# The guarded sum of a softmax row, moved from VectorE to ScalarE, with a new order of instructions

## The chip, the core and the metric

The kernel runs on one core of a Trainium2 chip. The core has five engines with instruction streams of their own, which wait for each other through semaphores: TensorE (PE) does matrix products and writes them to PSUM; its weight loads (PEld) run beside its products. VectorE (DVE) does reductions and elementwise work, ScalarE (ACT) activation functions of the form f(scale * x + bias), GpSimd (POOL) elementwise work on SBUF alone, and SyncE (SP) issues transfers between HBM and SBUF. Each engine runs its instructions in the order in which they were written; what stands first and must wait holds all behind it. The metric is the time of one launch on the device, in microseconds (us), as the median of several runs.

## The reference, cut to what matters

Eight batches, eight heads, 576 tokens, 64 values a head. Attention keeps only scores within tau of the row's maximum, and its result goes through a gated network with a convolution over three tokens.

```python
scores = scale * np.matmul(q, k.transpose(0, 1, 3, 2))
thresh = np.max(scores, axis=-1, keepdims=True) - tau
scores = np.where(scores >= thresh, scores, -1000000000.0)
scores = scores - np.max(scores, axis=-1, keepdims=True)
attn = np.exp(scores)
attn = attn / (np.sum(attn, axis=-1, keepdims=True) + 1e-09)
out = np.matmul(attn, v)                 # then, per batch, on all heads side by side:
h = np.maximum(x @ w_in, 0.0)            # 512 -> 1024
conv_out = sum over k of conv_w[k] * h shifted by k - 1 tokens
y = (h / (1 + np.exp(-conv_out))) @ w_out  # 1024 -> 512
```

The change touches the divisor: the sum of a row of exponentials plus a small guard.

## The kernel before

**Tiling.** A batch is cut in two chunks of query tokens, of 256 and 320 (L40, L284). A pair of heads is handled at a time; the first half of the keys of both lies on the lower 64 of the 128 partitions, the second half on the upper 64. A *unit* is 128 rows of queries for a pair (two heads, so two score tiles of 128 x 576); the last 64 rows of two pairs share a unit. There are 144 units, 18 a batch.

**One unit** (`unit`, L548). For each head h, PE makes the scores in PSUM (L569), DVE takes the row's maximum, negated (L581), and ACT takes the exponential with that as its bias (L588) into a tile `em`. DVE makes both thresholds (L585), then per head compares the scores with the threshold and multiplies the exponentials by the outcome, adding them up on the way (mask, L591). All these scalars lie in one tile `few` of 14 columns: the two sums in columns 4 and 6, and beside each, in 5 and 7, the guard, a constant written once (L319). The *guarded sum* is a DVE reduce over the pairs (4, 5) and (6, 7) that gives both heads at once, in columns 10 and 11 (L612); DVE takes their reciprocals in place (L615), and POOL, or DVE in a sixth of the first eight units' heads, scales `em` by them (L629). There are four `few` tiles and six `em` tiles, used in turn, and two score tiles in PSUM.

**After a unit** its `em` is turned so that keys lie on partitions: in 60 units by PE in blocks, with ACT copying them out of PSUM (L688, L698, L704), in 84 by splitting the words into halves on ACT and POOL (L337, L339), writing them to HBM (L666) and reading them back by two turning transfers (L673). When a group of two pairs has its turned blocks, `attend` makes the products with v (L724), ACT and DVE write them as a high and a low part (L732, L735). When a chunk has all of them, the network runs: first products (L754), Relu (L763), the two outer taps (L769), Tanh (L776), the gate (L774), high and low parts (L784, L344), second products (L805) and the copy to the output (L812). In the first stretch the weights are loaded and split as well (`split`, L365).

**The order.** No engine's order is written by hand. Each operation is registered with `op` (L102): engine, estimated ns, what it reads and writes, and `ahead`, the number of units by which it may run before its own unit's turn. `Plan.run` (L121) then plays all engines against each other: an engine that is free takes, of its operations that are ready and have a buffer, the one with the least rank minus `ahead` (L183 to L224). It uses estimates: LATENCY (from the end of an operation on one engine to its use on another), HOLD (a port shared by DVE and POOL), LATE (what is added for transfers), ALT (the handicap of an engine that is not an operation's home), and, on PE, SWITCH (cost of a change between 64-row work "rows", transposes "turn" and full-array work "full") with KEEP, how far past its due time PE may stay in the same form. The order found is the order written, on all engines at once, so one constant can shift every stream. MOE is read in `ffn` (L817) alone: how many first and second products alternate.

The lines of the sum before:

```python
        op("dve", 85, guard, w=[(few, "inverse")], r=ss, ahead=a)
        op("dve", 82, lambda: nc.vector.reciprocal(few[:, inverse], few[:, inverse]), w=[(few, "inverse")], ahead=a)
```

Of the kernel before, what the change touches and what calls it, by code (L numbers as in the profile page):

```python
# [16 lines left out]
AF = mybir.ActivationFunctionType  # L17
ALU = mybir.AluOpType
PSUM = bass.MemoryType.PSUM

LEAST = 2.0 ** -80
FEW = 4
AHEAD = {'mask': 16.335, 'norm': 7.023, 'parts': -3.757, 'gate': 1.809, 'evac': 0.518, 'low': 0.256, 's': 8.629, 's4': 9.599, 't': 3.039, 'a': 3.703, 'prep': 6.114, 'w': 0.866, 'load': 0.211, 'first': 6.092}

LATENCY = {'pe': 225.727, 'act': 201.983, 'dve': 114.993, 'pool': 52.585, 'ring': 1864.473}

HOLD = {'pool': 113.97, 'dve': 80.64}

NORM = (('pool', 'pool', 'pool', 'pool', 'pool', 'dve'), ('pool',))

# [1 line left out]
PIECES = 12  # L32
LOW = ('pool', 'pool')
HPB = 3
MOE = (2, 1)
BACKLOG = {'pool': 3000.0, 'dve': 1500.0, 'act': 9000000000.0}
WRATE = (1.997, 2.191)
ALT = 4.35

FIRST = [(0, 1), (2, 3, 4)]  # L40
GROUPS = [(0, 1), (2, 3, 4)]
# [18 lines left out]
STB = 3  # L60
ETB = 2
VAB = 3
QB = 2
CROSS = ((2, 1, 2, 1), (2, 1, 2, 1), (0, 0))
LATE = {'load': 1341.0, 'copy': 13872.0, 'rows': 132.0, 'turn': 331.0}

KEEP = {'rows': 3.312, 'cols': 0.001, 'turn': 0.039, 'full': 0.041}


class Buf:  # L70
# [184 lines left out]
def tile_tau_attention_gated_ffn(  # L255
# [13 lines left out]
    nc = tc.nc  # L269
# [34 lines left out]
    op = plan.op  # L304
# [13 lines left out]
    for x in fews:  # L318
# [3 lines left out]
            w=[(x, "tau")], r=[(x, 0), (tau_sb, 0)], ahead=8.0  # L322
# [9 lines left out]
    gate = const("gate", [P, 1], F32)  # L332
# [151 lines left out]
    ring = [const(f"g{i}", [P, NFB, RING], F32R) for i in "hl"]  # L484
# [63 lines left out]
    def unit(u, sides, small):  # L548
# [5 lines left out]
        few = plan.buf(sm, "few", FEW, [P, 14], F32, f"few_{u}")  # L554
        few.home = fews[few.turn % FEW]
        a = AHEAD["s4" if small else "s"]
        late, pss = [], []
        add = dict(op=ALU.add, axis=mybir.AxisListType.X)
        m = 2
        for h in range(m):  # L560
# [29 lines left out]
            def mask(scores=scores, th=th, view=view, total=total):  # L590
# [7 lines left out]
                r=[x for _, k, r in sides for x in ((k, h), *r(h))], ahead=a, kind="rows"  # L598
# [8 lines left out]
        ss = [(few, ("sum", h)) for h in range(m)]  # L607
        inverse = slice(10, 10 + m)
# [2 lines left out]
            pairs = few[:, 4:4 + 2 * m].rearrange("p (h two) -> p h two", two=2)  # L611
            nc.vector.tensor_reduce(few[:, inverse], pairs, **add)  # L612

        op("dve", 85, guard, w=[(few, "inverse")], r=ss, ahead=a)
        op("dve", 82, lambda: nc.vector.reciprocal(few[:, inverse], few[:, inverse]), w=[(few, "inverse")], ahead=a)  # L615
        turns = NORM[u >= NEAR]
        homes = [turns[(u * 2 + h) % len(turns)] for h in range(m)]
        if "act" in homes:
            op(
                "dve", 82, lambda: nc.vector.tensor_scalar(few[:, 12:12 + m], few[:, inverse], LEAST, None, op0=ALU.mult),  # L620
                w=[(few, "least")], r=[(few, "inverse")], ahead=a
            )
        for h, home in enumerate(homes):
# [227 lines left out]
    whole, made, vts, lasts, eTs = {}, {}, {}, {}, {}  # L851
# [8 lines left out]
    for now in range(len(units) + 1):  # L860
        plan.rank = float(now)
        if now < len(units):
            i, t, n = units[now]
# [106 lines left out]
```

## Time and profile before

| | |
|---|---|
| three timed runs | 836.83, 838.25, 838.29 us; median 838.25 |
| profiled execution | 836.68 us |
| its span, first to last instruction | 834.6 us |
| instructions | 20770 |
| mean granted clock of PE | 0.998 |
| HBM read and written | 47.34 MB, 58.98 MB |

The page of the profile and the answers drawn from its trace name an engine, a line (L612 is line 612 of the kernel), an operation with the tile that it writes and those that it reads, and a count. In a row of a group, the first number behind the bar is busy time in us, the second the mean of one instruction in ns, the third the idle time of the engine just ahead of these instructions, with what ended most of it. Operations of one engine overlap at their ends, so the length of one is more than the time for which it holds its engine; that is seen where two start one behind the other. Windows give busy times within a stretch of the span. Waits give who was waited for, the total in us, how often, and the longest. Idle time of an engine that is not the bottleneck costs nothing.

### The profile page before, as it was taken

To read this page: it belongs to the slowest core of one execution; us is meant where nothing else is said; L and a number is where in the kernel's file an instruction comes from. 1 tells how busy PE (TensorE), PEld (TensorE's weight loads), DVE (VectorE), ACT (ScalarE), POOL (GpSimd) and SP (SyncE) were. 2 spreads that over 40 slices of the span, in tenths; PEclk is the share of its full clock that TensorE was granted. 3 is DMA by queue.
4 is the path that set the end of the run, shared out by engine and by line. 5 is a ranking of instruction groups with operands and counts; after the bars stand their busy time and mean duration, and the time that the engine had idled before them with its cause. 6 is when DMAs were issued, how large, how long until landed. Compare 5 with 4: busy or idle time off the path is not lost.

```text
span 834.6 us, 20770 instructions
## 1 busy us (share of the span) xinstructions
PE 812.8 (97%) x7584; PEld 591.3 (71%) x7584; DVE 722.9 (87%) x1802; ACT 610.0 (73%) x1245; POOL 483.5 (58%) x631
## 2 busy tenths in 40 slices
PE   6889999999999999999999999999999999999998
PEld 2446767667777677767777677767777677777896
DVE  6999999989989699997989789997989879997542
ACT  5999787778777577876767777875867857776642
POOL 3456666755657357764756646674665637665321
PEclk9999999999999999999999999999999999999999
DMA  7446248999887789899898678889787887785301
GB/s 271 138 158 200 78 113 235 230 254 241 196 213 187 201 213 211 208 226 229 202 216 196 183 206 225 209 190 218 209 203 218 189 207 187 208 196 156 55 27 38
DMA packets 248550, 157.23 MB, mean 188 GB/s; under 512 B 203776, under 2 KB 222465, under 8 KB 248449
## 3 DMA queue, kind: packets, MB, share of 16 engines
q1 hardware_dynamic: 248016, 155.61, 72.5%
q8 instruction: 60, 0.98, 0.5%
q14 instruction: 42, 0.34, 0.1%
q10 hardware_dynamic: 432, 0.30, 0.1%
HBM read 47.34 MB, written 58.98 MB: 127 GB/s over the span
## 4 chain that ended last, share of the span: by engine, by line
PE 91%; DVE 4%; ACT 3%; issue 1%; POOL 0%; DMA 0%; DVEq 0%
PE po L805 24%; PE ph L754 24%; PE ps_s L569 18%; PE pa L724 16%; PE ps_t L688 7%; DVE few L581 2%; DVE em L591 1%; ACT em L588 1%; ACT eT L698 1%; DVE t L769 0%; PE pw_stage L415 0%; POOL em L629 0%; ACT stage L393 0%; ACT stage_f L389 0%; DMA k<-in_kp_dram 0%
## 5 line engine op out<-in xcount | busy, mean ns | idle before, releaser
L629 POOL TENSOR_SCALAR em<-em,few 128x576 f32<-128x576 f32 x285 | 227.0, 807 | 189.6 <-DVE few L615 147.0
L588 ACT ACTIVATE em<-ps_s,few 128x576 f32<-128x576 f32 x288 | 209.5, 744 | 68.1 <-DVE few L581 66.9
L581 DVE TENSOR_REDUCE few<-ps_s 128x1 f32<-128x576 f32 x288 | 209.2, 748 | 43.1 <-PE ps_s L569 41.3
L591 DVE SCALAR_TENSOR_TENSOR em<-ps_s,few,em 128x576 f32<-128x576 f32 x288 | 224.2, 811 | 13.1 <-ACT em L588 5.8
L754 PE MATMUL ph<-x,w1h 128*128 128x322 f32 (+1 forms) x1024 | 230.7, 304 | 0.8 <-ACT hp L763 0.8
L344 POOL TENSOR_TENSOR gl<-t,gh 128x255 fp32r<-128x255 f32 (+9 forms) x192 | 122.8, 651 | 109.1 <-ACT gh L784 102.7
L754 PEld LDWEIGHTS ph<-x,w1h 128*128 128x128 f32 x1024 | 170.6, 189 | 21.0 <-issue 15.2
L569 PE MATMUL ps_s<-k,q 64*64 64x288 f32 x2048 | 162.4, 424 | 8.5 <-DVE k L341 3.9
L724 PE MATMUL pa<-eT,v 64*64 64x256 f32 (+1 forms) x2304 | 152.5, 404 | 0.0
L754 PE MATMUL ph<-x,w1l 128*128 128x322 f32 (+1 forms) x512 | 150.9, 295 | 0.0
L724 PEld LDWEIGHTS pa<-eT,v 64*64 64x64 f32 x2304 | 88.7, 133 | 51.0 <-issue 3.2
L805 PE MATMUL po<-w2h,gh 128*128 128x512 f32 x288 | 119.2, 414 | 0.0
L569 PEld LDWEIGHTS ps_s<-k,q 64*64 64x64 f32 x2048 | 65.8, 134 | 68.5 <-issue 26.4
L805 PE MATMUL po<-w2h,gl 128*128 128x512 f32 x288 | 112.6, 391 | 0.0
L805 PE MATMUL po<-w2l,gh 128*128 128x512 f32 x288 | 112.6, 391 | 0.0
L769 DVE SCALAR_TENSOR_TENSOR t<-hp,cr 128x321 f32<-128x321 f32 (+1 forms) x128 | 88.4, 692 | 22.7 <-ACT hp L763 21.7
L339 POOL COPY parts<-em 128x1152 uint16<-128x1152 uint16 x84 | 101.9, 1213 | 3.9
L337 ACT ACTIVATE parts<-em 128x1152 uint16<-128x1152 uint16 x84 | 98.2, 1169 | 4.4 <-POOL em L629 4.1
L754 PEld LDWEIGHTS ph<-x,w1l 128*128 128x128 f32 x512 | 96.5, 188 | 0.3
L688 PE MATMUL ps_t<-ident,em 128*128 128x128 f32 x540 | 85.6, 284 | 8.7 <-ACT eT L698 5.0
L776 ACT ACTIVATE t<-t,cm 128x321 f32<-128x321 f32 (+1 forms) x128 | 68.6, 540 | 31.9 <-DVE t L769 19.9
L688 PEld LDWEIGHTS ps_t<-ident,em 128*128 128x128 f32 x540 | 61.6, 143 | 42.5 <-issue 19.7
(71 smaller groups left out, 871.7 us busy)
## 6 DMA issues: line engine op xcount, KB each, us to landing
rows<-parts SPq DMA_DIRECT2D x84, 576.0 KB, 3.6
q<-in_qd_dram SPq DMA_DIRECT2D x63, 256.0 KB, 4.0
v<-in_vc_dram SPq DMA_DIRECT2D x36, 288.0 KB, 4.4
out_dram<-ot SPq DMA_DIRECT2D x36, 256.0 KB, 3.8
k<-in_kp_dram SPq DMA_DIRECT2D x31, 288.0 KB, 4.8
stage<-in_w_in_dram SPq DMA_DIRECT2D x8, 512.0 KB, 5.3
stage<-in_w_out_dram SPq DMA_DIRECT2D x8, 512.0 KB, 4.0
eT<-rows SPq DMA_TRANSPOSE x168, 4.4
```

What stands on the lines that cost most here:

```text
L337: nc.scalar.activation(dst, src, AF.Copy, scale=scale)
L339: engines[e].tensor_copy(dst, src)
L344: engines[e].tensor_tensor(dst, x, y, op=ALU.subtract)
L569: nc.tensor.matmul(ps[g * D:(g + 1) * D, AT + c * CH:AT + (c + 1) * CH], lhsT=q(on, h), rhs=k[on, h * CH:(h + 1) * CH], start=True, stop=True)
L581: nc.vector.tensor_reduce(few[:, nm], scores(), op=ALU.max, axis=mybir.AxisListType.XY, negate=True)
L588: nc.scalar.activation(view(), scores(), AF.Exp, bias=few[:, nm])
L591: nc.vector.scalar_tensor_tensor(view(), scores(), few[:, th], view(), op0=ALU.is_ge, op1=ALU.mult, accum_out=few[:, total])
L629: engines[e].tensor_scalar(sl, sl, LEAST, few[:, 10 + h:11 + h], op0=ALU.add, op1=ALU.mult)
L688: nc.tensor.transpose(out=pt[:, i * P:(i + 1) * P], in_=block, identity=ident[:])
L724: nc.tensor.matmul(pa[j * D:(j + 1) * D, :w], lhsT=vt[on, step, :], rhs=eT[on, :w // D, step, :], start=(step == 0), stop=(step == NBLK - 1))
L754: nc.tensor.matmul(ph[:, :an], lhsT=w1[w][:, cb, fs], rhs=xs[cb][:, h, :an], start=(cb == 0 and i == 0), stop=(cb == NCB - 1 and i == 2))
L805: nc.tensor.matmul(po[:], lhsT=x[:, f, at:at + P], rhs=w[:, f, :], start=(f == 0 and i == 0), stop=(f == NFB - 1 and i == 2))
```

## The change

The sum with its guard becomes two activations, one a head: out = Identity(sum + bias), with the guard's column as the bias, written to columns 10 and 11. DVE's reciprocal then reads what both wrote. In the planner an activation is estimated at 112 ns and has a lead of `a + AHEAD["norm"]`, that is 8.629 + 5.208 units (9.615 + 5.208 in a unit of 64-row remainders). The branch on "act" in `homes` isn't reached, since NORM names POOL and DVE alone. The constants of the planner change as well: the leads in AHEAD, LATENCY, HOLD, ALT, LATE, KEEP and MOE.

```diff
-AHEAD = {'mask': 16.335, 'norm': 7.023, 'parts': -3.757, 'gate': 1.809, 'evac': 0.518, 'low': 0.256, 's': 8.629, 's4': 9.599, 't': 3.039, 'a': 3.703, 'prep': 6.114, 'w': 0.866, 'load': 0.211, 'first': 6.092}
-LATENCY = {'pe': 225.727, 'act': 201.983, 'dve': 114.993, 'pool': 52.585, 'ring': 1864.473}
-HOLD = {'pool': 113.97, 'dve': 80.64}
+AHEAD = {'mask': 18.575, 'norm': 5.208, 'parts': -4.059, 'gate': 1.956, 'evac': 0.512, 'low': 1.528, 's': 8.629, 's4': 9.615, 't': 3.024, 'a': 3.793, 'prep': 6.793, 'w': 0.762, 'load': 0.212, 'first': 6.093}
+LATENCY = {'pe': 235.362, 'act': 201.983, 'dve': 114.993, 'pool': 53.653, 'ring': 1862.277}
+HOLD = {'pool': 113.804, 'dve': 80.206}
...
-MOE = (2, 1)
+MOE = (1, 1)
-ALT = 4.35
+ALT = 6.24
...
+GUARD = "act"
-LATE = {'load': 1341.0, 'copy': 13872.0, 'rows': 132.0, 'turn': 331.0}
-KEEP = {'rows': 3.312, 'cols': 0.001, 'turn': 0.039, 'full': 0.041}
+LATE = {'load': 1389.0, 'copy': 16128.0, 'rows': 332.0, 'turn': -600}
+KEEP = {'rows': 3.535, 'cols': 0.001, 'turn': 0.02, 'full': 0.049}
...
-        op("dve", 85, guard, w=[(few, "inverse")], r=ss, ahead=a)
-        op("dve", 82, lambda: nc.vector.reciprocal(few[:, inverse], few[:, inverse]), w=[(few, "inverse")], ahead=a)
+        if GUARD == "act":
+            for h in range(m):
+                op(
+                    "act", 112, lambda h=h: nc.scalar.activation(
+                        few[:, 10 + h:11 + h], few[:, 4 + 2 * h:5 + 2 * h], AF.Identity, bias=few[:, 5 + 2 * h:6 + 2 * h]
+                    ), w=[(few, ("whole", h))], r=[(few, ("sum", h))], ahead=a + AHEAD["norm"]
+                )
+            ss = [(few, ("whole", h)) for h in range(m)]
+        else:
+            op("dve", 85, guard, w=[(few, "inverse")], r=ss, ahead=a)
+        op("dve", 82, lambda: nc.vector.reciprocal(few[:, inverse], few[:, inverse]), w=[(few, "inverse")], r=ss, ahead=a)
...
-                "dve", 82, lambda: nc.vector.tensor_scalar(few[:, 12:12 + m], few[:, inverse], LEAST, None, op0=ALU.mult),
+                "act", 110, lambda: nc.scalar.activation(few[:, 12:12 + m], few[:, inverse], AF.Copy, scale=LEAST),
```

## The prediction

> **What bounds the kernel now.** I read the busy times of the page first, then the chain that ended last, then the windows by stage, and last the waits of the stages in which TensorE (PE) is idle.
>
> ```profile
> PE 812.8 (97%) x7584; PEld 591.3 (71%) x7584; DVE 722.9 (87%) x1802; ACT 610.0 (73%) x1245; POOL 483.5 (58%) x631
> PE 91%; DVE 4%; ACT 3%; issue 1%; POOL 0%; DMA 0%; DVEq 0%
> 0.00:20.00 20.00, 11.94 (x83) 5.74 (x84) 13.51 (x38) 11.60 (x21) 6.09 (x22) 1.00 0.79 268
> 20.00:100.00 80.00, 71.76 (x673) 43.99 (x673) 77.36 (x193) 73.42 (x153) 49.67 (x55) 0.98 0.44 145
> 100.00:450.00 350.00, 349.03 (x3399) 254.74 (x3399) 319.73 (x805) 264.06 (x528) 215.96 (x275) 1.00 0.84 208
> 450.00:800.00 350.00, 348.94 (x3266) 258.94 (x3266) 297.59 (x745) 247.50 (x519) 203.89 (x273) 1.00 0.75 189
> 800.00:835.00 35.00, 31.13 (x170) 27.90 (x168) 14.69 (x24) 13.42 (x28) 7.89 (x8) 1.00 0.08 30
> ```
>
> A window row gives its length, then the busy time of PE, PE's weight loads, VectorE (DVE), ScalarE (ACT) and GpSimd (POOL), then granted clock, DMA share and GB/s. The shares of the first two rows say "PE", and the windows say where that holds. From 100 to 800 us PE is idle for 0.97 + 1.06 = 2.03 us in 700: whatever DVE gains there can only go to those 2 us and to the way in which PE's work is strung together. From 20 to 100 us it is otherwise: PE idles 8.24 us, DVE 2.64, ACT 6.58. There both are as full as PE. After 800 us the guarded sum no longer runs (its last row of the window view below), so that stretch cannot change by it.
>
> The start's own chain, by line, and the waits of the body (100 to 800 us), with us in total, number and longest:
>
> ```profile
> by line: DVE few L581 11.3%; PE pa L724 10.8%; PE ps_s L569 9.2%; DVE em L591 8.5%; ACT em L588 8.0%; PE ps_t L688 6.8%; ACT eT L698 6.1%; issue 5.8%; PE ph L754 5.8%; PE pw_stage L415 4.0%; ACT stage L393 3.6%; ACT stage_f L389 2.8%; ACT w
> PEld ps_s L569 <- issue: 23.2, 84, 0.5
> PEld ps_t L688 <- issue: 14.9, 34, 0.4
> PEld ph L754 <- issue: 14.7, 34, 0.4
> PEld po L805 <- issue: 7.3, 16, 0.5
> PEld pa L724 <- issue: 2.1, 9, 0.4
> PEld ps_t L688 <- POOL em L629: 2.5, 4, 1.1
> PE ps_t L688 <- POOL em L629: 0.7, 1, 0.7
> ```
>
> In the start the chain is a braid: DVE holds 11.3 + 8.5 = 19.8% with the row maximum and the mask, ACT at least 8.0 + 6.1 + 3.6 + 2.8 = 20.5% (the row is cut off; I take 22%). In the body what is left are 84 + 34 + 34 + 16 + 9 = 177 places where weight loads pause with nothing to wait for: there the matmul changes its form (64-row tiles, transposes, full array). What one costs PE is seen below.
>
> **The change, part by part.** Removed is the two-element reduce on DVE, once a unit; added are two one-element Identity activations a unit on ACT, and two hand-overs, DVE to ACT and back.
>
> ```profile
> L612 DVE TENSOR_REDUCE few<-few 128x2 f32<-128x4 f32 x144 | 21.4, 149 | 2.3
> 20.00:100.00 80.00, 2.12 (x14) 0.98 0.44 145
> 100.00:800.00 700.00, 18.82 (x127) 1.00 0.80 199
> 800.00:835.00 35.00, 0.00 (x0) 1.00 0.08 30
> 405.90 0.08 DVE L591 DVE_READ_ACCUMULATOR em<-ps_s,few,em 128x1 f32 x1
> 406.29 0.15 DVE L612 TENSOR_REDUCE few<-few 128x2 f32<-128x4 f32 x1
> 406.36 0.47 DVE L769 SCALAR_TENSOR_TENSOR t<-hp,cr 128x255 f32<-128x255 f32 x1
> 406.75 0.16 DVE L615 RECIPROCAL few<-few 128x2 f32<-128x2 f32 x1
> 407.09 1.64 POOL L629 TENSOR_SCALAR em<-em,few 128x576 f32<-128x576 f32 x2 [1.23 <-PE ps_s L569]
> ```
>
> The last five rows are start, length, engine and line. The reduce lasts 0.149 us, but the next operation starts 406.36 - 406.29 = 0.07 us after it: it holds DVE for 0.07, and 0.149 is the upper end. So DVE is relieved of 14 x 0.07 = 1.0 us (to 2.1) in the start and of 127 x 0.07 = 8.9 us (to 18.8) in the body.
>
> The trace has no Identity, so I build its price from what is nearest: a copy of one column, and two activations of 255 columns from the same memory, one with a per-partition operand and one without.
>
> ```profile
> L784 ACT ACTIVATE gh<-t 128x1 fp32r<-128x1 f32 x8 | 1.7, 211 | 0.1
> 529.75 0.74 ACT L588 ACTIVATE em<-ps_s,few 128x576 f32<-128x576 f32 x1
> 530.37 0.57 ACT L784 ACTIVATE gh<-t 128x1 fp32r<-128x1 f32 x2
> 398.18 0.42 ACT L784 ACTIVATE gh<-t 128x255 fp32r<-128x255 f32 x1
> 398.48 1.16 ACT L337 ACTIVATE parts<-em 128x1152 uint16<-128x1152 uint16 x1
> 409.78 0.53 ACT L776 ACTIVATE t<-t,cm 128x255 f32<-128x255 f32 x1
> 410.18 0.43 ACT L784 ACTIVATE gh<-t 128x255 fp32r<-128x255 f32 x1
> ```
>
> The 255-column copy holds ACT for 398.48 - 398.18 = 0.30 us, the Tanh, whose scale is a tile, for 410.18 - 409.78 = 0.40: the operand costs 0.10. Activations overlap: the exp lasts 0.74 and the next starts after 0.62, 0.12 earlier. A one-column copy lasts 0.211, so it holds ACT for 0.211 - 0.12 = 0.09. With the bias tile an Identity is 0.19; the ends are 0.09 (operand free) and 0.31 (0.21 + 0.10, nothing overlapped). The planner is told 0.112. ACT gets 288 x 0.19 = 54.7 us: 28 x 0.19 = 5.3 in the start (2.5 to 8.7), 254 x 0.19 = 48.3 in the body, where ACT is idle 85.94 + 102.50 = 188.4 us, so the body hides it; without that cover up to 48.3 us would be on the path.
>
> **Start, ACT.** Of 5.3 us I put on the path the share that ACT has of the start's chain, 22%: +1.2 (0 to +5.3). **Start, DVE**: 20% of 1.0: -0.2 (0 to -2.1). Before 20 us the first unit may gain or lose a few tenths by its order: 0.
>
> The Trainium skill, on the page "ScalarE: Activation LUTs", section "Rules for kernel authors", sends additions to VectorE and not to ScalarE. The rows bear it out for price (0.07 us a unit on DVE against 0.38 on ACT); by that rule alone nothing is gained and the start pays its 5.3, which is the slower rival below.
>
> **The longer hand-over.** Before, sum to reciprocal stays on DVE, and GpSimd starts the division 407.09 - 405.98 = 1.1 us after the last sum. Now an Identity pair stands between: behind it in ACT's strict order wait the next exp and the evacuations of PSUM, and behind the reciprocal on DVE wait the maxima that release exps and the masks that free the score banks. The two Identities take at least 0.19 + 0.31 = 0.5 us with their operands at hand, so division starts about 0.5 later per unit. PE felt GpSimd's division in 4 + 1 places of the body; 0.5 more in each is 2.5, most covered by the six buffers of em: +0.3 (-0.5, where the planner now sets the reciprocal sooner, to +2.5).
>
> **The body's DVE relief.** 8.9 us fewer on DVE, and masks with more lead (16.3 to 18.6 units), can take back what PE idles: of 2.0 us I take -1.6 (0 to -2.0).
>
> **The new order.** The price of one change of form on PE:
>
> ```profile
> 405.85 0.28 PE L754 MATMUL ph<-x,w1l 128*128 128x256 f32 x1
> 405.96 0.28 PE L754 MATMUL ph<-x,w1h 128*128 128x256 f32 x1
> 406.17 0.72 PE L569 MATMUL ps_s<-k,q 64*64 64x288 f32 x8
> ```
>
> Within a run the next matmul starts after 0.11, across the change after 0.21: 0.10 is lost. The planner may now stay in 64-row work 3.535 units past its due time, not 3.312, and in full-array work slightly longer. If one change in ten of the 177 goes, that is 18 x 0.10 = -1.8 (+3.5 to -3.5 for a fifth more or fewer, since nothing in the trace fixes the sign). MOE does nothing: in L829 to L833 all second-matmul items but one are already out before the loop that reads it, so its only effect is in how many first-matmul items each round takes, and their order stays. ALT prices engines other than an operation's home, and the trace has none used:
>
> ```profile
> L629 POOL TENSOR_SCALAR em<-em,few 128x576 f32<-128x576 f32 x285 | 227.0, 807 | 189.6 <-DVE few L615 147.0 <-PE ps_s L569 32.5 <-PE ps_t L688 7.1
> L629 DVE TENSOR_SCALAR em<-em,few 128x576 f32<-128x576 f32 x3 | 2.5, 834 | 0.0
> ```
>
> (285 + 3 divisions, as the homes say.) LATENCY and HOLD are estimates that only shift the order; LATE's copy is read nowhere; the ACT form of "least" isn't reached, as no home is "act".
>
> **DMA turns and loads.** LATE tells the planner that rows land 0.20 us later and turns 0.93 us earlier: attention may be put 0.73 earlier against its turned blocks. Loads of q, k and v get 0.68 unit more lead, and SP issues in order, so a load that waits for its buffer holds the turns behind it.
>
> ```profile
> eT<-rows SPq DMA_TRANSPOSE x168, 4.4
> SPq L511 <- PE ps_s L569: 34.4, 26, 3.6
> ```
>
> 168 turns are six for each of 28 attention groups; loads of q already wait 26 times for PE. Before, PE never idled ahead of pa, so I take 0 (0 to 28 x 0.73 = +20 if every group sat at its limit).
>
> **Sum.** +1.2 - 0.2 + 0.3 - 1.6 - 1.8 = -2.1. The profiled execution took 836.68 us (span 834.6 and 2.1 around it), so 834.6. The three timed runs have their median 1.57 us above it, at 838.25; carried there, 836.15, given as 836.2, which is 0.24% faster. This kernel's measurement tells about 0.2% (1.7 us) from no change; its own runs lie 1.5 apart.
>
> **Rivals.**
> - *ACT takes over the start* (slower). All 28 Identities land on the chain: 5.3 less the 1.0 of DVE, 838.25 + 4.3 = 842.5. It decides from where added ACT time plus the waits for sums exceeds ACT's 6.6 us idle there: 28 hand-overs of 0.05 each suffice. For it: ACT's 73.42 of 80 us, and a planner that counts 0.112 where rows give 0.19. Against: only a fifth of the chain is ACT's. Chance 0.19.
> - *The turns or the SP queue become a wait.* A quarter of the 0.73 in each of 28 groups is 5.1: 843.4. For it: the planner's shift; against: no wait of pa now. Chance 0.09.
> - *PE hides it all.* Body at 99.7% PE, start's plus and minus cancel: 836.6 to 839.9, nothing measurable. Chance 0.28.
> - *The order is much better.* A fifth of the form changes (-3.5), the 2.0 of idle, and a third of the start's 8.2 of PE idle (-2.7): 830.0. Chance 0.10.
> - *The change does not do what it says*, by a table load around each Identity. Chance 0.01, left out of the range:
>
> ```profile
> L330 ACT ACT_TABLE_LOAD x1 | 1.3, 1283 | 1.7 <-PEq L958 1.7
> ```
>
> One load of 1.283 us serves Exp, Tanh, Relu, Abs and Copy here; 288 of them would add some 370 us to ACT.
>
> **How the numbers follow.** The forecast, 1.7 to 5 us of gain (833.2 to 836.6), has 0.33. Faster: 0.33 + 0.10 = 0.43; same: 0.28; slower: 0.19 + 0.09 + 0.01 = 0.29. As both signs are likely, the range takes in both: 830, the better order, to 843, just above the ACT rival; a tenth is left out on either side.
>
> **What would show it.** L612 gone, 288 Identities of 0.21 to 0.31 us; DVE's busy time lower by 10 to 21 us, ACT's higher by 50 to 90. Right in its steps, if PE's idle time from 100 to 800 us falls below 2 us and the pauses by "issue" below 177. Wrong, if PE's busy time in the first 100 us falls behind 83.7 with ACT full there (first rival), if PE idles ahead of pa (second), or if the number of form changes grows.

## The result and the profile after

| | before | after |
|---|---|---|
| median of four timed runs, us | 837.95 (836.83 to 838.29) | 842.41 (841.89 to 842.94) |
| profiled execution, us | 836.68 | 842.04 |
| its span, us | 834.6 | 840.2 |

After over before is 1.0059, with a 95% interval of 1.0044 to 1.0074. The change makes the kernel slower by about 5 us. The forecast was 0.24% faster.

First the page of the kernel after: busy time by engine, and the shares of the chain that ended last.

```profile
PE 816.5 (97%) x7584; PEld 596.4 (71%) x7584; DVE 709.0 (84%) x1658; ACT 667.9 (80%) x1533; POOL 488.4 (58%) x631
PE 89%; ACT 7%; DVE 2%; POOL 1%; issue 1%; DMA 0%; ACTq 0%; DVEq 0%
```

DVE has 144 instructions fewer and is busy 13.9 us less; ACT has 288 more and is busy 57.9 us more, as foretold. In the chain ACT's share went from 3% to 7%. Where that is, the windows of the kernel after show (length, then PE, PEld, DVE, ACT, POOL, then granted clock, DMA share, GB/s):

```profile
0.00:20.00 20.00, 11.15 (x82) 5.13 (x82) 12.95 (x33) 12.55 (x26) 5.95 (x21) 1.00 0.80 270
20.00:100.00 80.00, 69.54 (x643) 40.15 (x639) 73.95 (x176) 76.28 (x174) 51.51 (x54) 0.98 0.45 142
100.00:450.00 350.00, 349.38 (x3394) 256.48 (x3390) 311.08 (x731) 290.57 (x660) 216.16 (x274) 1.00 0.81 207
450.00:800.00 350.00, 349.72 (x3289) 262.18 (x3282) 296.28 (x697) 274.52 (x645) 206.85 (x276) 1.00 0.76 191
800.00:841.00 41.00, 36.66 (x195) 32.48 (x193) 14.70 (x24) 14.02 (x29) 7.90 (x8) 1.00 0.09 33
```

From 100 to 800 us PE is idle for 0.62 + 0.28 = 0.90 us; it was 2.03. By that sign the body is better. But at 800 us PE has 36.66 us of work left, and had 31.13 before: it is 5.5 us late. In the first 100 us PE was busy 11.15 + 69.54 = 80.69 us (83.70 before), ACT 88.83 (85.02 before).

PE's network products date the loss more directly than busy time. The window 0 to 100 us of the tile ph (first products; PE, PEld, ACT, then clock, DMA share, GB/s), for the kernel before and then the one after:

```profile
0.00:100.00 100.00, 12.23 (x81) 10.24 (x81) 2.87 (x6) 0.98 0.51 170
```

```profile
0.00:100.00 100.00, 9.41 (x63) 7.88 (x63) 2.50 (x5) 0.98 0.52 167
```

And the answer on the tile po, whose two times are the first and the last start of a second product, again before and then after:

```profile
L805 PE MATMUL po<-w2h,gh x288: 387/393/504, 104.6 to 830.3; 128*128 128x512 f32 x144
```

```profile
L815 PE MATMUL po<-w2h,gh x288: 387/393/504, 110.1 to 835.8; 128*128 128x512 f32 x144
```

By 100 us PE has issued 63 matmuls of the first products where it had issued 81. The first second product comes at 110.1 and not at 104.6, the last at 835.8 and not at 830.3: 5.5 late at the one, 5.5 late at the other, with 725.7 us between them in both kernels. **The loss is there by 110 us, and the body neither adds to it nor takes any of it back.** The chain of waits in the stretch 20 to 100 us of the kernel after, by line, shows what the start now hangs on:

```profile
by line: ACT em L589 11.6%; PE pa L734 10.9%; PE ps_s L570 9.2%; ACT eT L708 9.2%; ACT stage_f L390 7.2%; ACT stage L394 5.9%; POOL stage_f L403 5.1%; PE pw_stage L416 3.9%; ACT few L618 3.8%; issue 3.5%; ACT w2h L411 3.1%; DVE cr L464 2.9%
```

ACT now holds at least 11.6 + 9.2 + 7.2 + 5.9 + 3.8 + 3.1 = 40.8% of it, twice the 20.5% of before, and the maximum and the mask on DVE have gone from its head. The Identities themselves are 3.8%. Such shares are no measure of load, though: experiments 3, 4 and 14 show how unsteady they are. What remains to be told apart is whether ACT's added time made it so, or the new order.

### The profile page after: what moved, and what is told of

Same layout as the page of the kernel before. It is cut to its first block, busy times and chain, and to the rows that moved or that the text cites. A ratio compares the mean times of both kernels' runs of the same rounds, so it can differ in the third digit from the quotient of the medians.

```text
span 840.2 us, 20888 instructions
## 1 busy us (share of the span) xinstructions
PE 816.5 (97%) x7584; PEld 596.4 (71%) x7584; DVE 709.0 (84%) x1658; ACT 667.9 (80%) x1533; POOL 488.4 (58%) x631
## 4 chain that ended last, share of the span: by engine, by line
PE 89%; ACT 7%; DVE 2%; POOL 1%; issue 1%; DMA 0%; ACTq 0%; DVEq 0%
PE ph L764 24%; PE po L815 24%; PE ps_s L570 18%; PE pa L734 15%; PE ps_t L698 7%; ACT em L589 2%; ACT eT L708 1%; ACT stage_f L390 1%; ACT stage L394 1%; ACT few L618 1%; DVE few L582 1%; ACT parts L338 1%; POOL em L639 0%; POOL stage_f L403 0%; PE pw_stage L416 0%
## 5 line engine op out<-in xcount | busy, mean ns | idle before, releaser
L639 POOL TENSOR_SCALAR em<-em,few 128x576 f32<-128x576 f32 x286 | 231.1, 819 | 190.6 <-DVE few L625 164.2
L589 ACT ACTIVATE em<-ps_s,few 128x576 f32<-128x576 f32 x288 | 207.4, 748 | 50.2 <-DVE few L582 48.5
L345 POOL TENSOR_TENSOR gl<-t,gh 128x255 fp32r<-128x255 f32 (+14 forms) x191 | 125.5, 667 | 115.4 <-ACT gh L794 105.4
L734 PEld LDWEIGHTS pa<-eT,v 64*64 64x64 f32 x2304 | 91.8, 133 | 48.4 <-issue 2.9
L570 PEld LDWEIGHTS ps_s<-k,q 64*64 64x64 f32 x2048 | 68.0, 134 | 66.2 <-issue 30.6
L338 ACT ACTIVATE parts<-em 128x1152 uint16<-128x1152 uint16 x84 | 98.3, 1170 | 16.5 <-POOL em L639 16.4
L779 DVE SCALAR_TENSOR_TENSOR t<-hp,cr 128x321 f32<-128x321 f32 (+1 forms) x128 | 84.1, 659 | 24.8 <-ACT hp L773 23.5
L618 ACT ACTIVATE few<-few 128x1 f32<-128x1 f32 x288 | 85.5, 305 | 19.4 <-DVE em L592 18.1
```

The costliest lines, as they stand in the source:

```text
L338: nc.scalar.activation(dst, src, AF.Copy, scale=scale)
L345: engines[e].tensor_tensor(dst, x, y, op=ALU.subtract)
L570: nc.tensor.matmul(ps[g * D:(g + 1) * D, AT + c * CH:AT + (c + 1) * CH], lhsT=q(on, h), rhs=k[on, h * CH:(h + 1) * CH], start=True, stop=True)
L589: nc.scalar.activation(view(), scores(), AF.Exp, bias=few[:, nm])
L639: engines[e].tensor_scalar(sl, sl, LEAST, few[:, 10 + h:11 + h], op0=ALU.add, op1=ALU.mult)
L734: nc.tensor.matmul(pa[j * D:(j + 1) * D, :w], lhsT=vt[on, step, :], rhs=eT[on, :w // D, step, :], start=(step == 0), stop=(step == NBLK - 1))
```

## The experiments

In most of them the order is *frozen*: the planner plays with one kernel's operations, estimates and constants, so all streams stay where they are, and only the instruction emitted at the place of the sum is another. So order and instruction can be told apart. All ratios are to the kernel before on the same chip, with their 95% intervals; those of the experiments come from five rounds. The numbers behind "first" and "last" are the first and last start of a second product, as in the rows above, in one profiled run each; the timed runs of one kernel lie up to 3.8 us apart (experiment 11), in most under 2, so small differences say little there.

| | sums in the start (17 units) | in the body | ratio | first to last, us |
|---|---|---|---|---|
| before | DVE | DVE | 1 | 104.6 to 830.3 |
| 3, old order | ACT | DVE | 1.0043 | 108.7 to 834.6 |
| 4, old order | DVE, and ACT loaded | DVE | 1.0044 | 108.5 to 834.0 |
| 13, old order | DVE, and ACT loaded | the same | 1.0048 | 107.6 to 834.9 |
| 9, old order | ACT | ACT | 1.0093 | 108.0 to 838.8 |
| 14, old order | no sum | no sum | 0.9981 | 103.9 to 828.1 |
| 10, new order | DVE | DVE | 1.0038 | 109.8 to 834.1 |
| 2, new order | ACT | DVE | 1.0066 | 111.8 to 836.4 |
| 1, new order | DVE | ACT | 1.0074 | 111.2 to 837.3 |
| after | ACT | ACT | 1.0059 | 110.1 to 835.8 |

### 1 and 2: the new order, with the sums of one stage back on DVE

The first of a unit's two places stays empty; at the second stands the old reduce (for all units before the 18th, or for all from it on).

```diff
...
+            seen = []
...
+            def whole_sum(h):
+                if u < 17:          # experiment 2: u >= 17
+                    seen.append(h)
+                    if len(seen) == m:
+                        guard()
+                else:
+                    nc.scalar.activation(few[:, 10 + h:11 + h], few[:, 4 + 2 * h:5 + 2 * h], AF.Identity, bias=few[:, 5 + 2 * h:6 + 2 * h])
...
```

> The changed kernel's order of instructions is kept; only in the first 17 units (those of the first 100 us) the guarded sum is the old reduce on VectorE, put where the second Identity stood. Theory 'ScalarE is the bound of the start': the 34 Identities of 0.185 us each no longer hold it, so most of the 4.4 us by which PE's work lags at 90 us comes back: about 838.0 to 839.5. Rival 'the new order itself is slower in the start': nothing comes back, 841.5 to 843. Rival 'the hand-over between VectorE and ScalarE costs it everywhere': a seventh or less comes back, 841.5 or more.

> The changed kernel's order is kept; the Identities stay in the first 17 units, and the other 127 units have the reduce on VectorE. Theory 'ScalarE is the bound of the start': the body is TensorE's, nothing changes, 841.5 to 843.0. Rival 'the hand-over costs everywhere': it is gone in 127 of 144 units, so 838 to 839. Rival 'the new order itself': 841.5 to 843 as well.

Measured: 843.22 us, 1.0074 (1.0060 to 1.0087), and 842.24 us, 1.0066 (1.0054 to 1.0078). With the body's sums on ACT, taking the Identities out of the start of the new order gives nothing back (from after to 1: +0.15%). With the body's sums on DVE the same step does give something: from 2 to experiment 10, below, 0.28%, 2.3 us. So what the start's Identities cost in the new order has no single size, and part of experiment 1's time may be the granted clock's (last section). Either way the first second product stays 5.2 to 7.2 us late, so the simple form of the first rival, 28 Identities on the start's chain, is not the whole of what the new order shows.

### 3 and 4: the old order, with ACT loaded in the start

Experiment 3 emits the two Identities where the reduce stood. Experiment 4 keeps the reduce and adds two Identities of constants into columns that nobody reads: ACT gets the time, nobody gets a wait.

```diff
-        op("dve", 85, guard, w=[(few, "inverse")], r=ss, ahead=a)
+        op("dve", 85, whole_sums if u < 17 else guard, w=[(few, "inverse")], r=ss, ahead=a)     # 3, whole_sums: both Identities
...
+        def guard_and_load():                                                                   # 4
+            guard()
+            for h in range(m):
+                nc.scalar.activation(few[:, 12 + h:13 + h], few[:, 5 + 2 * h:6 + 2 * h], AF.Identity, bias=few[:, 5 + 2 * h:6 + 2 * h])
+        op("dve", 85, guard_and_load if u < 17 else guard, w=[(few, "inverse")], r=ss, ahead=a)
```

> The old kernel's order is kept; in the first 17 units the reduce is replaced, where it stood, by the two Identities on ScalarE. Theory 'ScalarE is the bound of the start': slower than before by up to 34 x 0.185 = 6.3 us, 840.5 to 844. Rival 'the new order itself': unchanged, 837 to 839. Rival 'the hand-over': slower too, and by more than e4.

> The old kernel's order and its reduce on VectorE are kept; in the first 17 units ScalarE makes two Identities more, of constants, whose result nobody reads, so they take its time and nobody waits for them but what stands behind them on ScalarE. Theory 'ScalarE is the bound of the start': the time of ScalarE alone does the harm, as much as in e3, 840.5 to 844. Rival 'the hand-over': 837 to 839, clearly faster than e3. Rival 'the new order itself': 837 to 839.

Measured: 840.49 us, 1.0043 (1.0031 to 1.0055), and 840.36 us, 1.0044 (1.0031 to 1.0057). The two are alike. Experiment 3 also relieves DVE of its reduce, so in the start the wait between DVE and ACT costs nothing that shows beyond that relief; ACT's own time does, 0.44%, 3.7 us. The chain of waits from 20 to 100 us in experiment 4, by line:

```profile
by line: ACT em L588 10.5%; ACT eT L703 10.2%; issue 8.4%; ACT stage_f L389 7.8%; DVE few L581 6.9%; ACT stage L393 6.4%; DVE em L591 5.6%; PE pa L729 5.6%; ACT few L617 3.8%; PE ps_s L569 3.3%; ACT k L337 3.2%; ACT w2h L410 2.8%; PE pw_sta
```

ACT holds at least 10.5 + 10.2 + 7.8 + 6.4 + 3.8 + 3.2 + 2.8 = 44.7%, in an order in which its rows came to 20.5% and were taken as 22%. That looks as if the load had made the start's chain ACT's own. Experiment 14, further down, has the same order with no load on ACT at all and is the fastest of these; its chain of waits over the same stretch:

```profile
by line: ACT em L588 15.4%; ACT eT L698 9.3%; ACT stage_f L389 7.8%; ACT stage L393 7.3%; PE ph L754 6.3%; issue 5.8%; PE pa L724 5.6%; DVE few L581 5.2%; PE ps_t L688 4.6%; DVE em L591 4.6%; ACT w2h L410 4.2%; PE ps_s L569 3.8%; ACT w1l L4
```

There ACT holds at least 15.4 + 9.3 + 7.8 + 7.3 + 4.2 = 44.0%, and in experiment 10, which starts late, 6.6 + 6.4 + 4.4 + 2.9 = 20.3%. With several engines nearly full, the chain may run through one or the other, and its shares say little of what added time will cost. The 3.7 us are shown by the edit, not by the chain.

### 5, 6 and 7: planned anew with one half of the change

Experiment 5 has the new constants with the sum on DVE, 6 the old constants with the sum on ACT, 7 the kernel after with the Identity estimated at 190 ns in place of 112; each is planned anew, so the order moves.

```diff
-GUARD = "act"
+GUARD = "dve"                          # 5
...
-                    "act", 112, lambda h=h: nc.scalar.activation(
+                    "act", 190, lambda h=h: nc.scalar.activation(      # 7
```

> The new constants, with the guarded sum on VectorE as before; the order is found anew for that. Theory 'the new constants make a slower start': as slow as the changed kernel or within 1 us of it, 1.004 to 1.007 of the kernel before. Rival 'the sum on ScalarE, taken into the planning, makes the order slower': the new constants alone are as good as the old, 0.998 to 1.002.

> The old constants, with the guarded sum on ScalarE; the order is found anew for that. Theory 'the new constants make a slower start': only ScalarE's load is added, which a new order can partly give way to: 1.000 to 1.003. Rival 'the sum on ScalarE makes the order slower': 1.004 to 1.007, as the changed kernel.

> The changed kernel with one number changed: the planner counts 190 ns for an Identity, near the 185 that it holds ScalarE, not 112. Theory 'the planner fills ScalarE in the start with 2.5 us more than it can do': 1.5 to 3 us faster than the changed kernel, 1.002 to 1.004. Rivals 'the constants' and 'ScalarE's load itself': no better than the changed kernel, 1.005 to 1.008.

Measured: 847.36 us, 1.0119 (1.0105 to 1.0133); 850.52 us, 1.0158 (1.0144 to 1.0171); 859.45 us, 1.0259 (1.0243 to 1.0275). All three lie outside every range that was expected, and the last shows it most: telling the planner a price near what the trace shows made the order worst of all. Every one of these orders is worse than both kernels, by more than any price in the change. The constants are not measurements that may be corrected one at a time; together with the placement of the sum they select one order. So 5 and 6 say nothing of the sum's own cost.

### 8: a small shift of the order, as a control

```diff
-HOLD = {'pool': 113.97, 'dve': 80.64}
+HOLD = {'pool': 113.804, 'dve': 80.206}
```

> A control: the kernel before with HOLD alone set to the new values (113.804 and 80.206 ns for 113.97 and 80.64), which says nothing about the sum and yet gives another order on all engines. If the time depends on parts of the change that one can name: 0.999 to 1.001. If any new order costs or gains some us by chance: outside of 0.998 to 1.002, and then differences of that size between new orders are no evidence for a cause.

Measured: 836.27 us, 0.9990 (0.9981 to 0.9999). With one constant changed slightly the old order stays nearly what it was (in the two traces PE has 6 instructions in another place, ACT 5, the others none), and so does the time. So it is no control for what an order as different as the new one costs by chance.

### 9, 10 and 13: the whole kernel in a frozen order

Experiment 9 has the edit of 3 in all units, 13 that of 4 in all units, 10 that of 1 in all units.

> The old kernel's order, with the reduce replaced, where it stood, by two Identities on ScalarE in all 144 units: the move alone, with no new order. Theory 'ScalarE's load harms only the start, the body is TensorE's': as in e3, 1.003 to 1.006 of the kernel before. Rival 'the hand-over harms the body too': beyond e3 by more than its interval, 1.008 or more.

> The changed kernel's order with the reduce on VectorE in all units, where the second Identity stood: the new order alone, without the move. Theory 'the new order is slower by itself': 1.004 to 1.008, no better than the changed kernel. Rival 'the move costs it, in the new order too': 0.998 to 1.002.

> The old kernel's order with its reduce on VectorE; in all 144 units ScalarE makes two Identities of constants more, which nobody waits for but what stands behind them on ScalarE. Theory 'in the body the hand-over costs (VectorE waits for ScalarE and back), in the start ScalarE's time': as e4, 1.003 to 1.006 of the kernel before. Rival 'ScalarE's time costs in the body too': as e9, 1.008 to 1.011.

Measured: 845.10 us, 1.0093 (1.0078 to 1.0108); 840.29 us, 1.0038 (1.0026 to 1.0050); 840.99 us, 1.0048 (1.0035 to 1.0060).

Experiment 10 tells the order's own part. It has the old instructions in the new order, and is 0.38% slower than before: 3.2 us, for the order alone. Its windows:

```profile
0.00:20.00 20.00, 11.38 (x78) 5.54 (x82) 12.88 (x34) 11.04 (x20) 5.91 (x21) 1.00 0.77 257
20.00:100.00 80.00, 68.17 (x649) 39.41 (x642) 77.33 (x192) 71.42 (x146) 51.61 (x54) 1.00 0.45 146
100.00:450.00 350.00, 349.77 (x3395) 257.70 (x3393) 317.03 (x801) 266.69 (x530) 216.04 (x274) 1.00 0.80 207
450.00:800.00 350.00, 349.80 (x3285) 261.96 (x3285) 299.44 (x754) 250.99 (x522) 206.19 (x275) 1.00 0.75 191
800.00:845.00 45.00, 34.91 (x187) 31.04 (x185) 14.70 (x24) 13.42 (x28) 7.90 (x8) 0.96 0.08 30
```

PE's idle time in the body is 0.23 + 0.20 = 0.43 us, the least of all, and still 34.91 us of work are left at 800 us. PE was busy 79.55 us in the first 100, with ACT at only 82.46 of 100: less ACT than before, and a later start. So in the new order the late start is not ACT's time but the places of the work. PE's busy time lacks most from 40 to 60 us (14.31 against 16.57 before) and from 80 to 100 us (17.27 against 19.03). One wait is new there: PE waits once, up to 49.3 us, for a piece of the weights' preparation on POOL, as it does in the kernel after and does not in the kernel before. The row of experiment 10, from 41 to 92 us (total, number, longest):

```profile
PE pw_stage L416 <- POOL stage_f L403: 1.4, 1, 1.4
```

The last of these pieces is late too. The last step of the preparation on POOL, from the answers on the tile stage_f for before, after and experiment 10, in this order (the two times are the first and the last start):

```profile
L402 POOL TENSOR_TENSOR stage_f<-stage_f,stage x16: 1286/1300/1555, 17.1 to 88.1; 128x512 int32<-128x512 int32 x16
```

```profile
L403 POOL TENSOR_TENSOR stage_f<-stage_f,stage x16: 1279/1297/1487, 17.7 to 95.1; 128x512 int32<-128x512 int32 x16
```

```profile
L403 POOL TENSOR_TENSOR stage_f<-stage_f,stage x16: 1275/1294/1507, 18.0 to 94.7; 128x512 int32<-128x512 int32 x16
```

The last of them comes 7.0 and 6.6 us later, and 6.5 and 8.6 later in experiments 1 and 2. The second products need it, but the first of them does not wait for it: in experiment 10 the weights made from it are done by 98.3 us, the first second product starts at 109.8, and from 92 to 108 us PE is busy without a gap. In experiment 15 the piece is as early as before (88.0) and the first second product still 2.4 us late. So PE is late with the work ahead of it, and only the 1.4 us of the wait are named here.

Experiments 9 and 13 give the price of the hand-over where the order isn't made for it. The difference of 9 and 13 is 0.45%, 3.8 us: both have the same load on ACT, only 9 makes the reciprocal wait for it. It is the price net of DVE's relief, since 13 keeps the reduce as well. ACT's time in the body costs nothing that shows (13 against 4: 1.0048 and 1.0044). The windows of the body and the end, first of 13, then of 9:

```profile
100.00:450.00 350.00, 348.39 (x3389) 254.64 (x3389) 317.61 (x800) 285.98 (x662) 215.60 (x275) 1.00 0.83 207
450.00:800.00 350.00, 349.50 (x3283) 258.60 (x3283) 303.31 (x757) 271.68 (x646) 207.21 (x277) 1.00 0.78 191
800.00:845.00 45.00, 35.70 (x190) 31.66 (x189) 14.69 (x24) 13.59 (x29) 7.89 (x8) 0.97 0.08 30
```

```profile
100.00:450.00 350.00, 347.96 (x3354) 253.63 (x3354) 307.64 (x730) 286.50 (x659) 211.72 (x272) 1.00 0.81 207
450.00:800.00 350.00, 348.37 (x3312) 257.29 (x3305) 299.38 (x701) 275.69 (x646) 207.53 (x278) 1.00 0.79 191
800.00:845.00 45.00, 39.65 (x208) 34.96 (x206) 15.19 (x25) 14.88 (x32) 9.39 (x12) 0.98 0.08 30
```

PE idles 2.11 us in the body of 13 and 3.67 in that of 9, which is 1.6 of the 3.8; where the rest goes these rows don't show. The waits of the body (100 to 800 us: total, number, longest), first of 9, then of the kernel after, show where the hand-over is:

```profile
DVE few L621 <- ACT few L616: 18.7, 32, 1.1
...
ACT few L616 <- DVE em L591: 13.9, 37, 0.7
```

```profile
ACT few L618 <- DVE em L592: 16.5, 44, 0.7
...
DVE few L625 <- ACT few L618: 10.9, 25, 0.9
```

The new order lets DVE's reciprocal wait 10.9 us for ACT where the old one lets it wait 18.7. ACT's own wait for the sums is not shorter, 16.5 against 13.9. That the new plan sets other work of DVE between is likely, but the rows show the waits alone.

### 11 and 12: ACT relieved in the start

Seven scalings of the keys that ACT makes in the start go to POOL, in both orders, to see whether relief of ACT brings back what load takes.

```diff
-                    copy(e, x(), x(), 0.125)
+                    copy("pool" if e == "act" and 10e3 < plan.now < 95e3 else e, x(), x(), 0.125)
```

> The kernel before, its order kept, with the sum on VectorE; the seven scalings of keys that ScalarE makes in the start, 7 x 0.573 = 4.0 us, are made by GpSimd, which is a third idle there. Theory 'ScalarE is a bound of the start': a part comes off, 0.996 to 0.999. Rival 'what ScalarE loses there only matters when it gets more, since VectorE is as full': 0.9985 to 1.0015. If GpSimd is late with the divisions instead: over 1.002.

> The changed kernel, its order kept, with the same scalings of keys of the start on GpSimd: ScalarE gets back about as much time as the Identities of the start took, without any change to the sum and its hand-over. Theory 'ScalarE's load is what the changed kernel pays in the start': 1 to 4 us faster than the changed kernel, 1.001 to 1.005 of the kernel before. Rival 'the new order pays elsewhere': 1.005 to 1.008, as the changed kernel.

Measured: 838.64 us, 1.0022 (1.0013 to 1.0030), and 845.21 us, 1.0095 (1.0082 to 1.0108). Both are slower: 0.22% against before, and about 0.36% against after; the second is above every range that was expected. The windows of experiment 11, the first 100 us:

```profile
0.00:20.00 20.00, 11.55 (x71) 5.33 (x71) 12.76 (x35) 10.08 (x17) 8.96 (x23) 1.00 0.78 265
20.00:100.00 80.00, 69.94 (x656) 41.37 (x655) 75.28 (x189) 69.09 (x142) 55.66 (x57) 1.00 0.44 141
```

The scalings became a load on POOL instead, which has 8.96 + 55.66 = 64.62 us of work against 6.09 + 49.67 = 55.76 before, and PE is behind, at 81.49 us against 83.70. As a test of ACT's part the pair is inconclusive.

### 14: no sum at all, in the old order

The guard is left out of the divisor, and the reciprocal reads the sums in columns 4 and 6. A row's largest exponential is about 1 and is never masked, so the divisor lacks 1e-09 of at least about 1.

```diff
-        op("dve", 85, guard, w=[(few, "inverse")], r=ss, ahead=a)
-        op("dve", 82, lambda: nc.vector.reciprocal(few[:, inverse], few[:, inverse]), w=[(few, "inverse")], ahead=a)
+        op("dve", 85, lambda: None, w=[(few, "inverse")], r=ss, ahead=a)
+        op("dve", 82, lambda: nc.vector.reciprocal(few[:, inverse], few[:, 4:4 + 2 * m:2]), w=[(few, "inverse")], ahead=a)
```

> The old kernel's order, in which the guarded sum is left out and the reciprocal reads the two sums as they are: VectorE is relieved of 144 reduces, ScalarE gets nothing. It leaves the guard out of the divisor. It bounds what the change could have gained by its relief. Theory 'the body is TensorE's, and the start is shared by several engines': 0.997 to 1.000. Rival 'VectorE's relief of 10 us reaches the end': 0.990 to 0.995.

Measured: 835.19 us, 0.9981 (0.9972 to 0.9990). All that the relief of DVE is worth in the old order is 0.19%, 1.6 us (0.8 to 2.3 by the interval). This version is faster than both kernels.

### 15 and 16: the old start with the rest in the new order

The order is written out as a list: what the old plan puts into its first 100 us, then the rest as the new plan has it. Experiment 15 has all sums on DVE, 16 has them on ACT from the 18th unit on.

```diff
+        order = [(int(x[:-1]), names[x[-1]]) for x in ORDER.split(";")]
...
+        for i, e in order:
...
+            self.ops[i][2](e)
```

> An order put together: what the old plan begins in its first 100 us, in its order, and then all that is left in the order of the changed kernel's plan; the sum on VectorE in all units. Theory 'the new order loses in its start alone': 0.998 to 1.002 of the kernel before. Rival 'the new order loses in the body, or by chance wherever orders meet': 1.003 or more.

> The order of e15, with the sum on ScalarE from the 18th unit on, as in the changed kernel, and on VectorE before. Theory 'a plan made for the Identities keeps their cost in the body to 1 or 2 us': 1.001 to 1.003 of the kernel before, 1 to 2 us over e15. Rival 'VectorE's relief gains in the body that was planned for it': faster than e15, 0.995 to 0.999.

Measured: 839.08 us, 1.0024 (1.0015 to 1.0033), and 840.42 us, 1.0039 (1.0026 to 1.0052). The start is mended, by the window 0 to 100 us of ph in experiment 15, and then the first and last second product there:

```profile
0.00:100.00 100.00, 12.05 (x81) 10.16 (x81) 2.43 (x5) 1.00 0.52 170
```

```profile
L708 PE MATMUL po<-w2h,gh x288: 387/393/505, 107.0 to 832.5; 128*128 128x512 f32 x144
```

81 matmuls of the first products by 100 us, as before. Yet it does not get below before: 2.0 us of loss come back behind 100 us, and they are there by the first second product (107.0, 2.4 late, and 2.2 late at the last). That was a miss, since 0.998 to 1.002 had been expected. Either the seam costs them, or the new order's stretch behind 100 us does; the two aren't told apart. It does tell that a good start cannot simply be put ahead of a given body. From 15 to 16 the Identities of the body cost 0.15%, within the uncertainty of both.

## Why the prediction was wrong, point by point

**Two steps failed: "The new order", -1.8, and the move itself, which the terms for the start, the hand-over and DVE's relief put at +1.2 - 0.2 + 0.3 - 1.6 = -0.3.** All were priced on the kernel before. Against it the new order with the old instructions costs +3.2 us (experiment 10), and the move in the old order +7.8 (experiment 9). Both parts have the other sign than forecast, and they may not be added up, as the sum below shows.

**"The new order", -1.8.** Its +3.2 lies near the far end that the term had (+3.5). The price was built from changes of form on PE in the body. The pauses of the weight loads there, in the kernel after:

```profile
PEld ps_s L570 <- issue: 25.5, 94, 0.5
...
PEld ph L764 <- issue: 12.6, 29, 0.5
...
PEld po L815 <- issue: 6.6, 15, 0.5
...
PEld ps_t L698 <- issue: 6.6, 15, 0.4
...
PEld pa L734 <- issue: 2.9, 10, 0.4
```

94 + 29 + 15 + 15 + 10 = 163, against 177. These are only the pauses for which no engine is named, and they are not the changes of form. With the pauses for which one is named, 246 in the body before are 241 after; and in the order of the matmuls in the traces PE changes its form 371 times there before, and 367 times after and in experiment 10. Of the 18 changes that were to go, 4 went, worth 0.4 us at the prediction's 0.10 each. Both signs that the prediction named for "right in its steps" came true, the idle time below 2 us and the pauses below 177, and the kernel was slower. They watched the body, while the order was paid for in the start, where the prediction had put no price on it: the term had no row for the first 100 us. The sign named for "wrong", PE's busy time in the first 100 us below 83.7, is the one that told. It told less cleanly than thought: experiment 14, faster than before, has 82.84 there. The number of first products by 100 us and the time of the first second product are better signs.

**Start, ACT: +1.2, mis-sized.** An Identity's price was right. ACT's timeline in the kernel after (start, length):

```profile
67.85 0.30 ACT L618 ACTIVATE few<-few 128x1 f32<-128x1 f32 x1
68.05 0.59 ACT L420 ACTIVATE w2l<-pw_stage 128x512 fp32r<-128x512 f32 x1
68.59 0.29 ACT L618 ACTIVATE few<-few 128x1 f32<-128x1 f32 x1
68.79 0.66 ACT L390 ACTIVATE stage_f<-stage 128x512 f32<-128x512 f32 x1
```

It lasts 0.30 us and holds ACT for 0.20 (67.85 to 68.05, 68.59 to 68.79); 0.19 had been estimated. The Trainium skill, page "ScalarE: Activation LUTs", section "What ACT_TABLE_LOAD costs", gives about 280 ns for an activation with a bias tile, beside its elements, and an overlap of about 93 ns with the next; the trace's 0.30 and 0.10 agree. What was wrong is the share that lands. In the old order the 34 Identities of the first 100 us (34 x 0.20 = 6.8 us) cost 3.7, more than half (experiment 4), and not the 22% that ACT had of the chain. The share of a chain in one trace is no price for time added: in the same order it is at least 20.5% before, 44.7% with the load (experiment 4) and 44.0% with no load and a faster kernel (experiment 14). The bound of 5.3 held.

**The first rival had the time and not the cause.** It gave 842.5, and 842.41 was measured. In the old order its mechanism is there (experiments 3 and 4), at 3.7 us. In the new order, which is the one that the change has, taking the start's Identities away again brings nothing or 2.3 us (after to 1, 2 to 10), and without any Identity the start is as late (experiment 10). That 842.5 and 842.41 agree is luck: one cause was priced at 4.3, two others make up the 4.9, and the base of 838.25 was the median of three runs, where later medians of 11 to 20 runs are 836.45 to 837.27.

The Trainium skill, page "ScalarE: Activation LUTs", section "Rules for kernel authors", sends additions to VectorE. The times agree where all sums move, in the old order (before and 9, 0.93%) and in the new (10 and after, 0.21%). Where the new order has half of the sums on each engine, experiments 1 and 2, it is no faster than after, so the loss is not one price.

**The longer hand-over: +0.3, mis-sized.** It was hidden by PE in the prediction's view. In the body of the old order it costs 3.8 us, net of DVE's relief, beyond the upper end of 2.5. In the new order the whole move, hand-over and load, costs the ratio of after to experiment 10: 0.21%, 1.8 us, with some 0.2% of uncertainty.

**The body's DVE relief: -1.6, and -0.2 in the start.** The size was right as a whole: with nothing in its place the relief is worth 1.6 us (experiment 14). It comes only when nothing takes the place of the sum.

**Turns, SP, MOE: 0, right.** In the body one weight load ahead of pa waits for a turned block, for 0.4 us and on ACT's copy, and no wait of PE there ends on a transfer. The loads of q do wait longer for PE's scores, 52.9 us against 34.4. Putting MOE back leaves the instructions of all five engines as they are. **ALT: right for the old order, wrong as a claim on the new.** There two operations run away from home: one division (POOL has 286, and 285 before) and the one in this group (DVE, where this line is otherwise POOL's). Their worth was not tried.

```profile
L345 DVE TENSOR_TENSOR gl<-t,gh 128x128 fp32r<-128x128 f32 x1 | 0.6, 619 | 0.0
```

**The sum as the runs show it.** The whole change is +4.9 us (0.59% of 837). There are two ways to divide it. With the order first, it is +3.2 for the order and +1.8 for the move within it. With the move first, it is +7.8 for the move in the old order (0.93%) and -2.9 for the new order after that. Neither is the right one: the two parts cost 3.2 and 7.8 alone, 11.0, and 4.9 together, because each was worth something different beside the other. The prediction took them as terms of one sum. The new order is a repair for the new placement, and the old placement needed none. Of the 7 us between the -2.1 of the forecast and the +4.9, about 5 belong to the order and about 2 to the move by the first way.

**What stays open.** Which constant makes the start of the new order late was not tried, nor whether any other order as different would be as late; the lead of the weights, "w", which went from 0.866 to 0.762, is a candidate and no more. Whether the 2 us of experiment 15 are the seam's, and whether relief of ACT would bring back in the old order what load takes, are open too.

## What to carry to other kernels

When a change comes with a new order, freeze the order and swap the instruction, and then keep the instruction and swap the order: the two runs beside the two kernels show what each part costs and whether they add up, and a plan made anew from half of the constants shows neither. Price added time in a stage where several engines are full by up to all of it, not by the engine's share of the chain in one trace, because that share moved from 20.5% to 44.0% here without any load. Make sure that what is counted is what has the price: the 177 pauses with no named engine were not PE's changes of form. Signs of success must watch every stage that the change touches: here the body's idle time and pauses improved while the start lost more.

## What was not expected of the hardware

Time on an engine cost as much as a wait for it: experiment 4, in which nobody waits for the added Identities, loses 0.44%, and experiment 3, in which the reciprocal waits for them and DVE has its reduce taken off, 0.43%.

The granted clock dips in some runs and not in others, and what a dip costs depends on where it falls. Before and after both show 0.98 from 20 to 100 us, and by shorter windows 0.91 from 40 to 60 us, where PE is idle for 3.4 of 20 us in the kernel before; experiment 10 shows 1.00 there and is still slower than before. Of the 20 timed runs of the kernel before beside experiments 13 to 16, the five with a mean granted clock of 1.000 have a median of 836.97 us and the 15 below it one of 836.79.

In experiment 1 the dip of the profiled run comes from 80 to 100 us. Its windows there, and then those of experiment 10, which up to this point has the same order and the same instructions:

```profile
80.00:100.00 20.00, 17.19 (x169) 11.02 (x169) 19.46 (x39) 14.72 (x35) 13.68 (x13) 0.91 0.13 31
```

```profile
80.00:100.00 20.00, 17.27 (x185) 11.50 (x184) 19.97 (x40) 14.86 (x35) 14.20 (x14) 1.00 0.20 56
```

PE is busy for the same time and gets 16 matmuls fewer done, and the first second product is 1.4 us later (111.2 and 109.8). The three timed runs of experiment 1 with the lowest mean clock (0.993 to 0.996) took 843.04 to 844.51 us, the other three 841.15, 841.16 and 843.41, so part of its 1.0074 is likely the clock's. These are single windows and few runs; they show that a dip can cost where PE has no idle time to spare, not how much it costs in general.
